# Two heads of q first, setup work moved, weights loaded earlier, and filler matmuls in the early attention units of a fused attention and expert kernel

## The chip, the cores and the metric

The kernel runs on one core of a Trainium2 chip. The metric is the device time of one execution in microseconds. Before the change three runs gave 231.26, 233.02 and 235.55 us; the median, 233.02 us, is the time before. A profile shows one execution, with a span of 231.7 us.

## What is computed

The first half is block attention with 4 batches, 8 heads, 768 rows, 64 columns per head, and 8 blocks of 96 rows. An 8x8 matrix per head is normalised five times (Sinkhorn), and the blocks of k and v are mixed with it. Each block of q then attends to its own mixed block. The second half is a layer of 8 experts: each of the 3072 rows, now 512 wide, goes to one expert.

```python
P = sort_net
for _ in range(5):
    P = exp(P - max(P, -1)); P = P / (sum(P, -1) + 1e-9); P = P / (sum(P, -2) + 1e-9)
k_sorted = einsum('bhij,bhjcd->bhicd', P, k_b)
v_sorted = einsum('bhij,bhjcd->bhicd', P, v_b)
attn = softmax(q_b @ k_sorted.T / 8)            # per block
x = (attn @ v_sorted)                           # rearranged to 3072 x 512
logits = x @ w_gate + modality_bias[modality_id]
e = argmax(logits); gate = max(softmax(logits))
out[row] = gate * (relu(x[row] @ w1[e]) @ w2[e])
```

With the biases of this input, nearly all rows go to two experts. The kernel finds the two likely ones on the chip and handles their rows in slots of 256 rows; whatever is left over goes through a general loop behind a branch.

## The kernel before

The instruction order is fixed by hand: each engine executes what the source issues, in that order. Attention goes in 32 units of four blocks for two batches. Unit `u` does `scores` (8 matmuls into PSUM), `expo` (one exponential on ScalarE), and, one unit later, `av` (8 matmuls, then a division on VectorE into `xb`).

```python
def scores(u):
    g, hf, h = unit(u)
    sc = scpsum.tile([128, 2, 512], FP32, tag="sc", ...)      # one buffer
    for j in range(4):
        for par in range(2):
            nc.tensor.matmul(sc[0:m, par, j * BLK:(j + 1) * BLK], kT[g][rows, x0:x0 + m], qT[rows, i],
                             start=True, stop=True)
def expo(u):
    mark[0] = nc.scalar.activation(attnT[u % 2]..., sc_tiles.pop(u)[0:BLK, :, 0:4 * BLK], ACT.Exp, scale=scale)
def av(u):
    op = opsum.tile([128, 2, 512], FP32, tag="op", ...)       # one buffer
    ...                                                        # 8 matmuls, reciprocal, multiply into xb
```

`BLK` is 96, so the scores use columns 0 to 383 of each of the two 512-column banks. `spread_q` interleaves the q of two heads in SBUF (two copies), `tq_pe` transposes one head on TensorE (6 transposes), and `tq_out` copies the result to `qT`. `sort_k` and `sort_v` do the mixing: matmuls with `bd` (the normalised matrix as a block diagonal), called `ka` and `va` in the profile. Group `g` holds two of the four batches.

The start, and the work between the first units:

```python
    load_q(0, 0)                      # four heads of q
    ...                               # iota, identity
    load_k(0, 0); load_k(0, 1); load_v(0); load_q(0, 1)
    ...
    spread_q(0, 0, nc.gpsimd); spread_q(0, 1, nc.gpsimd)
    ...
    for u in range(4):
        tq_pe(u)
    # five Sinkhorn iterations, make_bd(0), sort_k of group 0
    scores(0); expo(0)
    home_pick(); home_map()           # the two likely experts, on VectorE
    mod_rows()                        # modality ids: a copy, a transpose on TensorE, a copy
    load_k(1, 0); load_k(1, 1)
    wait_w = gate_consts()            # gate weights and biases, mostly on GpSimd
    make_bd(1)
    scores(1); expo(1)
    late_consts()                     # small constants on VectorE
    ...                               # sort_v of group 0 (12 jobs, three in a row: two small, one large)
    load_v(1); load_q(1, 0); load_q(1, 1)
    zero_block(); av(0); wait_w(); prep_s(4)
```

Per group of 8 units, `gate_T` and `gate_L` compute the logits, `choose` the expert, `place` each row's position, and `ones_[m](t)` scatters one set of rows to a DRAM scratch (GpSimd, one indirect DMA each). `table(m)` then works out which slots are ready, and `x_try` loads a slot's rows back with a transposing DMA (`xT`, issued by SyncE). The expert layers run as pieces: `mL1` (8 matmuls of 256 columns, `hp`) and `mL2` (8 matmuls of 512 columns, `yp`). Slots alternate between the two experts.

```python
    at2(9, place, 0)
    for t in range(1, 8):
        at1(9 + t, lambda t: ones_[0](t), t)
        if t == 3:
            at1(9 + t, lambda: load_w(0, parts=(0,)))
    at1(16, table_x, 0)
    at1(16, lambda: load_w(0, parts=(1,)))
    at1(16, lambda: load_w(1))
    ...
    for u in range(2, 32):
        p1, p2 = pace(u)              # (0, 0) before unit 18, then (1, u % 2)
        scores(u); expo(u)
        for f, a in A1.get(u, []): f(*a)
        run_pieces(p1)
        av(u - 1); prep_q(u + 2); prep_s(u + 3)
        for f, a in A2.get(u, []): f(*a)
        run_pieces(p2)
    run_pieces(1); av(31); run_pieces(2); gate_T(3, 3); run_pieces(1); gate_L(3, 3); choose(3)
    run_pieces(2); place(3)
    for t in range(1, 8):
        run_pieces(2); ones_[3](t)
    table_x(3)
    run_pieces(1000)
```

Of the kernel before, what the change touches and what calls it, by code (L numbers as in the profile page):

```python
# [17 lines left out]
def kernel(  # L18
# [13 lines left out]
    nc = tc.nc  # L32
# [58 lines left out]
    def q_in(g, hh):  # L91
        base = q_in1 if g else v_sb[1].rearrange("p x d -> p (x d)")
        return base[:, hh * 3072:(hh + 1) * 3072]
# [19 lines left out]
    def load_v(g):  # L113
        nc.gpsimd.dma_start(out=v_in, in_=v_src[g * 128:(g + 1) * 128])

    def load_q(g, hh):
        t = q_in(g, hh).rearrange("p (r h f) -> p r h f", r=2, h=4)
        return [nc.gpsimd.dma_start(out=t[:, par], in_=q[2 * g + par, 4 * hh:4 * hh + 4]
                                    .rearrange("h (p t) d -> p h (t d)", t=6)) for par in range(2)][0]

    def spread_q(g, hq, eng=None):
        t = q_in(g, hq // 2).rearrange("p (r h t d) -> p r h t d", r=2, h=4, t=6)
        il = q_il[hq % 2].rearrange("p (h t r d) -> p h t r d", h=2, t=6, r=2)
        for z in range(2):
            (eng or nc.vector).tensor_copy(il[:, z], t[:, :, (hq % 2) * 2 + z].rearrange("p r t d -> p t r d"))  # L125
# [1 line left out]
    sI = singles.tile([128, 32], I32)  # L127
    pI = singles.tile([128, 1], I32)
    idI = singles.tile([BLK, NTL], I32)
    load_q(0, 0)  # L130
    nc.gpsimd.iota(sI, pattern=[[1, 32]], base=0, channel_multiplier=0)
    make_identity(nc, ident)
    load_k(0, 0)
    load_k(0, 1)
    load_v(0)
    load_q(0, 1)
    jI = singles.tile([1, 4], I32)
    hI = singles.tile([1, 4], I32)
    nc.gpsimd.iota(pI, pattern=[[0, 1]], base=0, channel_multiplier=1)
# [1 line left out]
    nc.gpsimd.iota(jI, pattern=[[1, 2], [0, 2]], base=0, channel_multiplier=0)  # L141
    nc.gpsimd.iota(hI, pattern=[[PR, 2], [CAP, 2]], base=0, channel_multiplier=0)
    spread_q(0, 0, nc.gpsimd)
    spread_q(0, 1, nc.gpsimd)

    ones_bf = singles.tile([128, 128], BF16)
    ones8 = singles.tile([128, E], FP32)
# [40 lines left out]
    def perm_mult(dst, srcs, nm):  # L188
        eng = nc.gpsimd if nm == "w" else nc.vector
        tmp = small.tile([128, 4, E, E], FP32, tag="ptmp", name=f"ptmp{nm}")  # L190
        a = bass.AP(tensor=srcs.tensor, offset=srcs.offset, ap=[srcs.ap[0], srcs.ap[1], [0, E], srcs.ap[2]])
        p_ = bass.AP(tensor=perm.tensor, offset=perm.offset, ap=[perm.ap[0], [0, 4], perm.ap[1], perm.ap[2]])
        eng.tensor_tensor(tmp, a, p_, ALU.mult)
        return lambda: nc.vector.tensor_reduce(dst, tmp, AX.X, ALU.add)
# [39 lines left out]
    def tq_out(u, eng):  # L234
        g, h = u // 16, u % 8
        qT = qTb[g][:, h * 768:(h + 1) * 768].rearrange("p (i t r) -> p i t r", i=NB, t=6)
        eng(qT, tq.pop(u).rearrange("p t (i r) -> p i t r", r=16))

    for u in range(4):
        tq_pe(u)  # L240
    for it in range(5):
        if it == 0:
            nc.vector.tensor_reduce(red, P_t, AX.X, ALU.max)
            nc.vector.tensor_tensor(P_t, P_t, red.broadcast_to([BH, NB, NB]), ALU.subtract)
        nc.scalar.activation(P_t, P_t, ACT.Exp)
        if it == 3:
            tq_out(0, nc.scalar.copy)
        if it == 4:
            for u in range(1, 4):
                tq_out(u, nc.scalar.copy)  # L250
        for f in gap[it]:
            f()
        nc.vector.tensor_reduce(red, P_t, AX.X, ALU.add)
        nc.vector.reciprocal(red, red)
        nc.vector.tensor_tensor(P_t, P_t, red.broadcast_to([BH, NB, NB]), ALU.mult)
        nc.vector.tensor_reduce(red, P_swap, AX.X, ALU.add)
        nc.vector.reciprocal(red, red)
        colb = bass.AP(tensor=red.tensor, offset=red.offset,
                       ap=[red.ap[0], [0, NB], red.ap[1]])
        nc.vector.tensor_tensor(P_bf if it == 4 else P_t, P_t, colb, ALU.mult)  # L260
# [34 lines left out]
    def mod_rows():  # L295
        src = modI.rearrange("b (r t w) -> b t r w", r=16, t=6)[:, :, :, 0]
        nc.vector.tensor_copy(modB, src)
        tp = mipsum.tile([128, 64], BF16, tag="mi", name="modT")
        nc.tensor.transpose(tp[0:BLK, 0:NTL], modB.rearrange("b t r -> b (t r)"), ident[0:NTL, 0:NTL])
        nc.vector.tensor_copy(modF, tp[0:BLK, 0:NTL])  # L300

    wgf = small.tile([128, 4, E], FP32, tag="wgf", name="wgf")

    def gate_consts():
        red_w = perm_mult(wgf, wg_sb, "w")
        nc.gpsimd.tensor_scalar(modN, modF, -1.0, 1.0, ALU.mult, ALU.add)

        def bb(r):
            t = BTp[0:BLK, r]
            return bass.AP(tensor=t.tensor, offset=t.offset, ap=[t.ap[0], [0, NTL], t.ap[1]])  # L310
        tmp = small.tile([BLK, NTL, E], FP32, tag="btmp", name="btmp")
        nc.gpsimd.tensor_tensor(biasm, modF.broadcast_to([BLK, NTL, E]), bb(1), ALU.mult)
        nc.gpsimd.tensor_tensor(tmp, modN.broadcast_to([BLK, NTL, E]), bb(0), ALU.mult)
        nc.gpsimd.tensor_tensor(biasm, biasm, tmp, ALU.add)

        def rest_w():
            red_w()
            nc.vector.tensor_copy(wgp, wgf)
        return rest_w

    busy = [0.0, 0.0]

# [54 lines left out]
        return u // 16, (u // 8) % 2, u % 8  # L377

    def prep_s(u):
        if 4 <= u < 32 and not (u // 8) % 2 and u % 2 == 0:  # L380
            spread_q(u // 16, (u % 8) // 2)
            use(dve=0.7)

    def prep_q(u):
        if 4 <= u < 32 and not (u // 8) % 2:
            tq_pe(u)
            tq_out(u, nc.scalar.copy if pick(0.8, 0.56) else nc.vector.tensor_copy)

# [2 lines left out]
    def scores(u):  # L391
        g, hf, h = unit(u)
        sc = scpsum.tile([128, 2, 512], FP32, tag="sc", name=f"sc{u}")
        qT = qTb[g][:, h * 768:(h + 1) * 768].rearrange("p (i f) -> p i f", i=NB)
        for j in range(4):
            i = hf * 4 + j
            x0 = (h * 8 + i) * BLK
            m = 128 if h * 8 + i < 63 else BLK
            for par in range(2):
                rows = slice(par * 64, (par + 1) * 64)  # L400
                nc.tensor.matmul(sc[0:m, par, j * BLK:(j + 1) * BLK],  # L401
                                 kT[g][rows, x0:x0 + m], qT[rows, i],
                                 start=True, stop=True)
        sc_tiles[u] = sc

    def expo(u):
        mark[0] = nc.scalar.activation(attnT[u % 2][:, 0:8 * BLK].rearrange("p (r f) -> p r f", r=2),  # L407
# [189 lines left out]
    def zero_block():  # L597
        ins = nc.sync.dma_start(out=xs_dram[ZR:ZR + PR].rearrange("(t p) w -> p t w", t=2), in_=zsrc2)
        in_xs_group(ins.ins)
        pads.append(ins.ins)  # L600
# [8 lines left out]
    def w_views(z):  # L609
        o = z * WCOL  # L610
        return (w01[:, o:o + 4 * F].rearrange("p (c f) -> p c f", c=4),
                w01[:, o + 4 * F:o + WCOL].rearrange("p (c f) -> p c f", c=8))

    def load_w(z, tab=None, n=None, parts=(0, 1)):
        tb, n = (etab, z) if tab is None else (tab, n)
        er = nc.values_load(tb[0:1, n:n + 1], engines=(PoolEng,), min_val=0, max_val=E - 1)
        v1, v2 = w_views(z)
        if 0 in parts:
            nc.gpsimd.dma_start(out=v1, in_=moe_w1[bass.ds(er, 1)].rearrange("o (c p) f -> p (o c) f", p=128))
        if 1 in parts:  # L620
            nc.gpsimd.dma_start(out=v2, in_=moe_w2[bass.ds(er, 1)].rearrange("o (c p) f -> p (o c) f", p=128))

    def stage_of(s):
        return 0 if s < 2 else 1 if s < 4 else 2 if s < 8 else 3
# [123 lines left out]
    expo(0)  # L748
    home_pick()
    home_map()  # L750
    mod_rows()
    load_k(1, 0)
    load_k(1, 1)
    wait_w = gate_consts()
    make_bd(1)
    scores(1)
    expo(1)
    late_consts()
    use(dve=-busy[1], act=-busy[0])
    for n, (f, g, x0, kd) in enumerate(g0[8:]):  # L760
        f(g, x0, kd)
    load_v(1)
    load_q(1, 0)
    load_q(1, 1)
    zero_block()
    av(0)
    wait_w()
    prep_s(4)

    st = {"tab": -1, "x": 0, "l1": 0, "done": 0, "pos": 0}  # L770

# [24 lines left out]
    def at2(u, f, *a):  # L796
        A2.setdefault(u, []).append((f, a))

    at2(8, lambda: nc.vector.memset(v_sb[1][:, :, D:D + 1], 1.0))
    for m in range(4):  # L800
        for c in range(4):
# [3 lines left out]
                at2(u, gate_L, m, c)  # L805
        if m < 3:
            at2(8 * m + 9, choose, m)
    at2(9, place, 0)
    for t in range(1, 8):
        at1(9 + t, lambda t: ones_[0](t), t)  # L810
        if t == 3:
            at1(9 + t, lambda: load_w(0, parts=(0,)))
    at1(16, table_x, 0)
    at1(16, lambda: load_w(0, parts=(1,)))
    at1(16, lambda: load_w(1))
    at1(18, place, 1)
    for t in range(1, 8):
        at2(17 + t, lambda t: ones_[1](t), t)
# [42 lines left out]
    for u in range(2, 32):  # L861
        p1, p2 = pace(u)
        scores(u)
        expo(u)
        for f, a in A1.get(u, []):
            f(*a)
        run_pieces(p1)
        av(u - 1)
        prep_q(u + 2)
        prep_s(u + 3)  # L870
        for f, a in A2.get(u, []):
            f(*a)
        run_pieces(p2)
    run_pieces(1)
    av(31)
    run_pieces(2)
    gate_T(3, 3)
    run_pieces(1)
    gate_L(3, 3)
    choose(3)  # L880
    run_pieces(2)
    place(3)
    for t in range(1, 8):
        run_pieces(2)
        ones_[3](t)
    table_x(3)
    run_pieces(1000)
# [75 lines left out]
```

## Time and profile before

| engine | busy us | share of the span | instructions |
|---|---|---|---|
| TensorE, matmuls | 164.9 | 71% | 2023 |
| TensorE, weight loads | 122.8 | 53% | 2023 |
| VectorE | 104.7 | 45% | 340 |
| ScalarE | 94.3 | 41% | 147 |
| GpSimd | 76.1 | 33% | 102 |

The mean granted TensorE clock is 0.846 of full speed. The core's DMA engines moved 27.67 MB, 119 GB/s over the span. A transposing load of a slot's rows took 3.4 us in the median from issue to landing and 16.0 us at most; a weight load of 1024 KB took 15.8 us in the median.

In the profile the engines are PE (matmuls), PEld (weight loads of TensorE), DVE (VectorE), ACT (ScalarE), POOL (GpSimd) and SP (SyncE); a q after a name means its sequencer. A tile's name tells the stage: `sc` scores, `op` the product with v, `tq` a transpose of q, `gt` and `lg` the gate, `ka` and `va` the mixing, `hp` and `yp` the expert layers, `xs_scratch` the scattered rows. A line of the timeline gives start and duration in us, engine, source line, operation, output and inputs, and in brackets the idle time before it and what ended that. Shares of busy time are averages over stages with different limits, so a stage is read by its own windows.

### The profile page before, as it was taken

To read this page: it belongs to the slowest core of one execution; us is meant where nothing else is said; L and a number is where in the kernel's file an instruction comes from. 1 tells how busy PE (TensorE), PEld (TensorE's weight loads), DVE (VectorE), ACT (ScalarE), POOL (GpSimd) and SP (SyncE) were. 2 spreads that over 40 slices of the span, in tenths; PEclk is the share of its full clock that TensorE was granted. 3 is DMA by queue.
4 is the path that set the end of the run, shared out by engine and by line. 5 is a ranking of instruction groups with operands and counts; after the bars stand their busy time and mean duration, and the time that the engine had idled before them with its cause. 6 is when DMAs were issued, how large, how long until landed. Compare 5 with 4: busy or idle time off the path is not lost.

```text
span 231.7 us, 5104 instructions
## 1 busy us (share of the span) xinstructions
PE 164.9 (71%) x2023; PEld 122.8 (53%) x2023; DVE 104.7 (45%) x340; ACT 94.3 (41%) x147; POOL 76.1 (33%) x102
## 2 busy tenths in 40 slices
PE   0265667995999600298889888999990999999600
PEld 0154565985889500286565657668660576674200
DVE  5868866657548660044566436233270133232100
ACT  2264445665577710075464626443341132322300
POOL 7621515000434420031633465337651031333300
PEclk9997587569569955569999999999998699999965
DMA  5999999990119399981215323594364642212200
GB/s 69 208 228 203 218 213 174 198 184 3 36 36 162 101 150 184 191 138 37 108 48 129 97 75 121 127 145 148 96 214 97 105 103 96 92 45 91 89 15 0
DMA packets 30129, 27.67 MB, mean 119 GB/s; under 512 B 18799, under 2 KB 25743, under 8 KB 29840
## 3 DMA queue, kind: packets, MB, share of 16 engines
q0 software_dynamic: 11760, 23.10, 45.7%
q1 hardware_dynamic: 18336, 4.16, 11.8%
q8 instruction: 18, 0.29, 0.6%
q14 instruction: 15, 0.12, 0.2%
HBM read 27.35 MB, written 10.52 MB: 163 GB/s over the span
## 4 chain that ended last, share of the span: by engine, by line
PE 54%; DVE 16%; DMA 13%; issue 5%; POOL 3%; ACT 2%; SPq 1%; POOLq 0%; DVEq 0%
PE hp L663 19%; PE yp L686 15%; DMA xT<-xs_scratch 10%; PE ka L349 3%; PE gt L433 3%; DVE xb L424 3%; PE va L358 3%; PE op L420 3%; PE sc L401 2%; PE lg L439 2%; DMA xs_scratch<-zpad 2%; PE tq L231 1%; POOL xs_scratch L510 1%; DMA xs_scratch<-xb,dest 1%; DVE v_sb L336 1%
## 5 line engine op out<-in xcount | busy, mean ns | idle before, releaser
L663 PE MATMUL hp<-xT,w 128*128 128x256 bf16 x384 | 50.1, 284 | 18.5 <-DMA xT<-xs_scratch 18.4
L510 POOL DMA_INDIRECT xs_scratch<-xb,dest x32 | 29.6, 925 | 68.5 <-issue 33.6
L663 PEld LDWEIGHTS <-w 128*128 128x128 bf16 x384 | 37.6, 102 | 27.1 <-issue 12.6
L677 POOL DMA_INDIRECT out_dram<-kvb,idg x25 | 24.6, 985 | 54.5 <-ACT kvb L673 27.3
L407 ACT ACTIVATE attnT<-sc 96x768 bf16<-96x768 f32 x32 | 25.8, 806 | 10.8 <-PE sc L401 10.6
L657 ACT ACTIVATE hT<-hp 128x512 bf16<-128x512 f32 x17 | 10.1, 596 | 35.7 <-PE hp L663 35.6
L686 PE MATMUL yp<-w,qT 128*128 128x512 bf16 x96 | 22.9, 383 | 0.0
L424 DVE TENSOR_TENSOR xb<-op,rs 96x512 bf16<-96x512 f32 x32 | 22.0, 687 | 1.7 <-DMA xs_scratch<-xb,dest 0.6
L686 PE MATMUL yp<-w,hT 128*128 128x512 bf16 x96 | 22.5, 379 | 0.0
L423 DVE RECIPROCAL rs<-op 96x8 f32<-96x8 f32 x32 | 6.4, 199 | 30.5 <-PE op L420 29.1
L673 ACT ACTIVATE kvb<-yp,idg 128x512 f32<-128x512 f32 x15 | 10.3, 687 | 21.5 <-PE yp L686 21.5
L231 PE MATMUL tq<-ident,q_il 128*128 128x128 bf16 x96 | 10.8, 270 | 10.7 <-POOL q_il L125 10.3
L420 PE MATMUL op<-v_sb,attnT 96*128 96x65 bf16 x256 | 15.1, 207 | 2.1 <-DVE v_sb L336 1.3
L358 PE MATMUL va<-bd,kvb 128*128 128x128 bf16 x128 | 14.6, 285 | 1.4 <-ACT v_sb L336 0.8
L675 DVE TENSOR_SCALAR kvb<-yp,idg 128x512 f32<-128x512 f32 x9 | 6.8, 751 | 19.5 <-PE yp L686 19.5
L401 PE MATMUL sc<-qT,kT 64*128 64x96 bf16 (+1 forms) x256 | 12.9, 228 | 3.0 <-issue 1.1
L420 PEld LDWEIGHTS <-attnT 96*128 96x128 bf16 x256 | 12.8, 107 | 4.2 <-DVE v_sb L336 1.4
L657 ACT ACTIVATE qT<-hp 128x512 bf16<-128x512 f32 x15 | 9.0, 597 | 14.1 <-PE hp L663 14.0
L336 ACT CAST v_sb<-va 96x512 bf16<-96x512 f32 (+1 forms) x20 | 11.9, 629 | 6.7 <-PE va L358 6.5
L433 PE MATMUL gt<-ident,xb 96*128 96x96 bf16 x128 | 9.8, 230 | 6.6 <-DVE xb L424 5.7
L686 PEld LDWEIGHTS <-qT 128*128 128x128 bf16 x96 | 9.3, 100 | 9.5 <-issue 0.5
L358 PEld LDWEIGHTS <-kvb 128*128 128x128 bf16 x128 | 13.2, 189 | 2.0 <-issue 1.8
(176 smaller groups left out, 213.2 us busy)
## 6 DMA issues: line engine op xcount, KB each, us to landing
w<-in_moe_w_dram POOLq DMA_DIRECT2D x4, 1024.0 KB, 15.8
kvb<-in_k_dram POOLq DMA_DIRECT2D x4, 768.0 KB, 12.1
kvb<-in_v_dram POOLq DMA_DIRECT2D x2, 1536.0 KB, 10.7
v_sb<-in_q_dram POOLq DMA_DIRECT2D x4, 384.0 KB, 14.6
q_in<-in_q_dram POOLq DMA_DIRECT2D x4, 384.0 KB, 13.2
xs_scratch<-zpad SPq DMA_DIRECT2D x3, 258.0 KB, 3.4
xs_scratch<-xb,dest POOLq DMA_INDIRECT x32, 2.6
out_dram<-kvb,idg POOLq DMA_INDIRECT x25, 2.9
```

The lines of the kernel that those rows point to most:

```text
L336: (nc.scalar.copy if pick(act, dve) else nc.vector.tensor_copy)(dst, src)
L358: nc.tensor.matmul(acc[:, z], v_cols[:, d0 + z], bd[g], start=True, stop=True)
L401: nc.tensor.matmul(sc[0:m, par, j * BLK:(j + 1) * BLK], kT[g][rows, x0:x0 + m], qT[rows, i], start=True, stop=True)
L407: mark[0] = nc.scalar.activation(attnT[u % 2][:, 0:8 * BLK].rearrange("p (r f) -> p r f", r=2), sc_tiles.pop(u)[0:BLK, :, 0:4 * BLK], ACT. ...
L420: nc.tensor.matmul(ov[:, par, j], attnT[u % 2][:, c0:c0 + 128], v_sb[g][0:BLK, par * 64 + h * 8 + i, 0:D + 1], start=True, stop=True)
L424: nc.vector.tensor_tensor(xt[:, :, h * D:(h + 1) * D].rearrange("p (r j) d -> p r j d", r=2), ov[0:BLK, :, :, 0:D], rs.broadcast_to([BLK, ...
L433: nc.tensor.transpose(tp[:, t], xb[m % 2][:, t, c * 128:(c + 1) * 128], ident[:BLK, :BLK])
L510: ins = nc.gpsimd.indirect_dma_start(out=xs_dram, out_offset=bass.IndirectOffsetOnAxis(ap=dest[:, t:t + 1], axis=0), in_=xt.bitcast(I32)[: ...
L657: mark[0] = nc.scalar.activation(dst, src, ACT.Relu)
L663: nc.tensor.matmul(hp[:, f], w_at(s, c * F + (2 * j + f) * 128, 128), xT_b[s % NX][:, c], start=(c == 0), stop=(c == 3))
L677: ins = nc.gpsimd.indirect_dma_start(out=out, out_offset=bass.IndirectOffsetOnAxis(ap=idg[:, t, 0:1], axis=0), in_=y, in_offset=None, boun ...
L686: nc.tensor.matmul(yp, hT_b[s % 2][:, fc, t * 128:(t + 1) * 128], w_at(s, 4 * F + fc * Dm, Dm), start=(fc == 0), stop=(fc == 7))
```

## The change

The change reorders the start and the middle, and adds matmuls whose results nothing reads:

- q comes in with two heads, then two, then four. Only two heads are spread and transposed at the start; the others of group 0 are spread on GpSimd between loads.
- The modality rows, the bias constants, the second block diagonal and the late constants move from in front of v's mixing to after it or into units 2 to 4.
- The first expert's weights are loaded before the units. The second expert's loads wait until the rows of slot 1 are in.
- `place(0)`, the scatters of group 0 and `table_x(0)` move by up to one unit; in each unit a piece runs ahead of the gate's work instead of behind it; at the end there is one piece between steps instead of two.
- In units 2 to 17 six matmuls of 128 columns go into columns 384 to 511 of the score tile. They multiply the identity with part of `kT`. They are meant to keep the array active.

```diff
-    load_q(0, 0)
+    load_q(0, 0, 2)
...
-    load_q(0, 1)
+    load_q(0, 2, 2)
+    load_q(0, 4, 4)
...
-    spread_q(0, 1, nc.gpsimd)
...
-    for u in range(4):
+    for u in range(2):
         tq_pe(u)
...
-        if 4 <= u < 32 and not (u // 8) % 2 and u % 2 == 0:
+        if 16 <= u < 32 and not (u // 8) % 2 and u % 2 == 0:
             spread_q(u // 16, (u % 8) // 2)
...
         sc_tiles[u] = sc
+        if 2 <= u < 18:
+            for z in range(6):
+                nc.tensor.matmul(sc[:, z % 2, 4 * BLK:512], ident, kT[0][:, 0:128], start=True, stop=True)
...
     home_map()
-    mod_rows()
     load_k(1, 0)
     load_k(1, 1)
-    wait_w = gate_consts()
-    make_bd(1)
+    wait_w = gate_w()
     scores(1)
     expo(1)
-    late_consts()
...
+    spread_q(0, 1, nc.gpsimd)
     load_v(1)
-    load_q(1, 0)
-    load_q(1, 1)
+    load_q(1, 0, 4)
+    load_w(0, parts=(0,))
+    load_q(1, 4, 4)
+    load_w(0, parts=(1,))
+    spread_q(0, 2, nc.gpsimd)
     zero_block()
+    prep_q(2)
     av(0)
+    prep_q(3)
     wait_w()
-    prep_s(4)
+    mod_rows()
...
+    def late_w1():
+        for i, ins in enumerate(load_w(1)):
+            if i == 0:
+                tc.add_manual_dep(ins.ins, xins[1].ins.name, SYNC, reason="rows of the first slots go ahead")
...
-    at2(9, place, 0)
+    at2(2, lambda: (gate_bias(), spread_q(0, 3, nc.gpsimd)))
+    at2(3, make_bd, 1)
+    at2(4, late_consts)
+    at1(10, place, 0)
     for t in range(1, 8):
-        at1(9 + t, lambda t: ones_[0](t), t)
-        if t == 3:
-            at1(9 + t, lambda: load_w(0, parts=(0,)))
-    at1(16, table_x, 0)
-    at1(16, lambda: load_w(0, parts=(1,)))
-    at1(16, lambda: load_w(1))
+        at2(9 + t, lambda t: ones_[0](t), t)
+    at2(16, table_x, 0)
+    at2(17, late_w1)
...
         expo(u)
+        run_pieces(p1)
         for f, a in A1.get(u, []):
             f(*a)
-        run_pieces(p1)
         av(u - 1)
         prep_q(u + 2)
         prep_s(u + 3)
+        run_pieces(p2)
         for f, a in A2.get(u, []):
             f(*a)
-        run_pieces(p2)
     run_pieces(1)
     av(31)
-    run_pieces(2)
+    run_pieces(1)
     gate_T(3, 3)
...
-    run_pieces(2)
+    run_pieces(1)
     place(3)
     for t in range(1, 8):
-        run_pieces(2)
+        run_pieces(1)
         ones_[3](t)
```

`gate_w` and `gate_bias` are the two halves of `gate_consts`, split.

More of the change, by code (lines that the diff above doesn't have):

```diff
@@ L114, in load_v, with load_q @@
         nc.gpsimd.dma_start(out=v_in, in_=v_src[g * 128:(g + 1) * 128])
[L116 to L119, printed above, removed]
+    def load_q(g, h0, nh):
+        t = q_in(g, h0 // 4).rearrange("p (r h f) -> p r h f", r=2, h=4)
+        z = h0 % 4
+        for par in range(2):
+            nc.gpsimd.dma_start(out=t[:, par, z:z + nh], in_=q[2 * g + par, h0:h0 + nh]
+                                .rearrange("h (p t) d -> p h (t d)", t=6))
     def spread_q(g, hq, eng=None):
@@ L248 @@
         if it == 4:
-            for u in range(1, 4):
-                tq_out(u, nc.scalar.copy)
+            tq_out(1, nc.scalar.copy)
         for f in gap[it]:
@@ L302, with gate_w, rest_w, gate_bias @@
     wgf = small.tile([128, 4, E], FP32, tag="wgf", name="wgf")
-    def gate_consts():
+    def gate_w():
         red_w = perm_mult(wgf, wg_sb, "w")
+        def rest_w():
+            red_w()
+            nc.vector.tensor_copy(wgp, wgf)
+        return rest_w
+    def gate_bias():
         nc.gpsimd.tensor_scalar(modN, modF, -1.0, 1.0, ALU.mult, ALU.add)
@@ L314, in gate_consts @@
         nc.gpsimd.tensor_tensor(biasm, biasm, tmp, ALU.add)
[L316 to L319, printed above, removed]
     busy = [0.0, 0.0]
@@ L384, in prep_q @@
     def prep_q(u):
-        if 4 <= u < 32 and not (u // 8) % 2:
+        if 2 <= u < 32 and not (u // 8) % 2:
             tq_pe(u)
@@ L617, in load_w @@
         v1, v2 = w_views(z)
+        res = []
         if 0 in parts:
-            nc.gpsimd.dma_start(out=v1, in_=moe_w1[bass.ds(er, 1)].rearrange("o (c p) f -> p (o c) f", p=128))
+            res.append(nc.gpsimd.dma_start(out=v1, in_=moe_w1[bass.ds(er, 1)].rearrange("o (c p) f -> p (o c) f", p=128)))
         if 1 in parts:
-            nc.gpsimd.dma_start(out=v2, in_=moe_w2[bass.ds(er, 1)].rearrange("o (c p) f -> p (o c) f", p=128))
+            res.append(nc.gpsimd.dma_start(out=v2, in_=moe_w2[bass.ds(er, 1)].rearrange("o (c p) f -> p (o c) f", p=128)))
+        return res
     def stage_of(s):
```

## The prediction

> **What bounds the kernel now.** I read the page's forty slices first. TensorE is busy 71% of the span, no engine is a plain bound, so the waits decide.
>
> ```profile
> PE   0265667995999600298889888999990999999600
> PEclk9997587569569955569999999999998699999965
> DMA  5999999990119399981215323594364642212200
> ```
>
> Each digit is 5.8 us. TensorE has two holes after the prologue: slices 15 to 16 (from about 84 us) and slice 31 (about 175 to 180 us). In both the clock falls to half, and in the first the DMA row is full. The table of waits names the cause of both, 12.6 us for the longer and, by difference from 18.4 us, 5.8 us for the other:
>
> ```profile
> PE hp L663 <- DMA xT<-xs_scratch: 18.4, 2, 12.6
> ```
>
> The chain of waits shows what stands before each:
>
> ```profile
> 77.86 2.68 DMA xs_scratch<-xb,dest
> 80.75 15.98 DMA xT<-xs_scratch
> 96.86 1.87 PE hp L663 x8
> ...
> 122.54 3.25 DMA xT<-xs_scratch
> ...
> 171.24 3.82 DMA xs_scratch<-zpad
> 175.19 4.67 DMA xT<-xs_scratch
> 179.91 3.59 PE hp L663 x16
> ```
>
> The same transposed load of one slot of rows takes 15.98 us at 80 us and 3.25 us at 122 us. The timeline around 80 us tells why: GpSimd issues three weight loads of 1 MB around it, after one more at 68.23.
>
> ```profile
> 78.91 0.94 POOL L621 DMA_DIRECT2D w<-in_moe_w_dram  x1
> 80.10 0.79 POOL L619 DMA_DIRECT2D w<-in_moe_w_dram  x1 [0.25 <-issue]
> 80.75 1.83 SPq L630 DMA_TRANSPOSE xT<-xs_scratch  x1
> 80.89 1.01 POOL L621 DMA_DIRECT2D w<-in_moe_w_dram  x1
> ```
>
> 3 MB at the 190 GB/s of those windows is 16 us: the rows come with the last of the weights. The second hole is another matter: table 3 is asked for at about 168 us, its pads and rows land at 179.9, twelve us later, and TensorE has work left only until 173.85.
>
> For the attention stage I cut the trace at multiples of 3.413 us from 10.01, because its clock record changes nowhere else:
>
> ```profile
> 40.73:44.14 3.41, 3.41 (x49) 2.90 (x49) 1.88 (x6) 2.74 (x4) 0.00 (x0) 0.50 1.00 203
> 47.56:50.97 3.41, 3.41 (x82) 3.07 (x79) 2.03 (x5) 2.67 (x4) 0.00 (x0) 0.50 1.32 206
> 71.45:74.86 3.41, 3.35 (x59) 3.05 (x57) 3.19 (x7) 2.65 (x5) 1.38 (x2) 1.00 1.12 207
> ```
>
> Columns: length, busy TensorE, weight load, VectorE, ScalarE, GpSimd, then clock. From 37.32 to 50.97 and 57.80 to 68.04 TensorE has no idle time and half a clock; from 68 on it has the full one, and VectorE and ScalarE set the pace.
>
> [...]
>
> **The change, part by part.** Set from the start of unit 4's scores (41.3 us) and of unit 18's (80.6 us).
>
> *Prologue.* Two heads of q instead of four come first, so k lands about 2 us sooner (0.39 MB less at 200 GB/s). But the first ka matmul at 15.57 waited for VectorE's bd, not for k: nothing won. [...] 192 ka at 30.5 ns are 5.9 us against 4.5, about 1 us lost. The modT transpose, which held TensorE until 25.2, moves behind v: 1 to 1.5 us won at the start of va; VectorE also loses 3 us of small work ahead of its v copies. But va hangs on four 16-row jobs that share one PSUM buffer (fill 0.5 to 0.9, copy 1.0 to 1.2, 0.3 between): 8 to 9 us in either kernel. So va ends about 1.2 us earlier, at 32.6. Then a new wait: unit 2 needs heads 4 and 5 spread, now on GpSimd, behind load_v (which waits for va), four q loads and two weight loads: 0.6 + 3.0 + 0.8 + 0.94 with gaps is 6 us, then 0.8 for the first copy, so 39.3. Before, that transpose ran at 37.4. With spreads and biases off VectorE later, I put unit 4 at 42.0: **+0.7**.
>
> *Fillers.* 16 units x 6 = 96 matmuls of 128 columns. Six transposes of the same shape advance the chain by 0.64 us at half clock and 0.34 at full: 107 and 56 ns each, so 10.3 us or 5.4 us of TensorE. In the order of instructions, the signal that the exponential waits for has moved from the last score matmul to the last filler, so they also lengthen the loop scores, exponential, next scores. [...] I take the full clock from about 42 us until the wait.
>
> *Units 4 to 17.* Against before: the half-clock units with k or v work, 5, 7, 6, 11, win 1.3, 0.2, 0.4, 0.75 (their matmuls halve, 0.34 of filler is added); light units 4, 8 and 16 lose 0.1, 0.3, 0.35; unit 13 loses 0.25. Unit 9 held TensorE 2.9 us for choose; place now stands after unit 10's scores, which wins 2.2 and costs 0.8 in unit 10. Table 0 goes behind unit 15's division: 0.5 won in unit 17. Together **-3.5**: scores of 18 at 77.8.
>
> *First rows.* The first expert's weights are loaded from 37 us and are in by about 60 (5.2 MB at 0.2 MB/us); the second's wait for slot 1's rows. From unit 16's exponential: scatter 0.3 + 0.9, landing 2.7, rows 3.3, so 7.2 us, while scores of 18 come 3.8 us after it: a wait of 3.4 to 3.7 us. Before, scores of 18 to the first hp was 96.86 - 80.56 = 16.3. **-12.6**.
>
> *Units 18 to 31.* The piece now precedes gate_T, which waited for VectorE's xb in seven units, like this one:
>
> ```profile
> 107.19 0.51 PE L433 MATMUL gt<-ident,xb 96*128 96x96 bf16 x8 [0.75 <-DVE xb L424]
> ```
>
> 7 x 0.7 = 4.9 won. Place 1, once hidden in the hole, costs 0.9; and slot 2's rows, just in time before, will be waited for by about 1.5. **-2.5**.
>
> *Tail.* Before table 3 the loop runs 21 pieces, then 20; now 11. Nine pieces at (4 x 0.88 + 2 x 1.73) / 6 = 1.17 us are 10.5 us more cover after it, and 5.8 us are needed: the second hole goes. With one piece instead of two, choose and place wait 1.2 us. **-4.8**.
>
> Sum: 0.7 - 3.5 - 12.6 - 2.5 - 4.8 = -22.7, and 233.0 - 22.7 = 210.3: I say **210 us**.
>
> **Rivals.** (1) *The clock does not follow.* If fillers leave it at half, they cost up to 10.3 us where TensorE is the pace: about 217. [...] (2) *A wait takes the first hole's place.* The second expert's 2 MB start after slot 1's rows, about 10.5 us after unit 16's exponential, and take 11; its first use is four units later, at about 20. GpSimd meanwhile stands at that load[...]. If this holds slot 1 or 2 back by 5 us: 215. (3) *GpSimd becomes the prologue's bound*, with seven issues and six copies in order: 3 to 4 us more, 214. (4) *The fillers were for nothing because units are bound by copies*: then units 4 to 17 win nothing, 214. Better than planned: half-clock windows at 97 to 102 gone as well, 3 us, 206.
>
> **Range and chances.** The two holes are 18.4 us of named waits. Each rival is some 4 to 7 us; two at once give about 221, none of them and the extra gain with some luck 201: range 201 to 221. All three rivals together give 226, still below the 228.4 that 2% asks for; only a hole that stays reaches it. Faster by over 2%: 0.94; within 2%: 0.04; slower: 0.02.
>
> **What would show it.** Rows of slot 0 landing 3 to 4 us after their issue, with TensorE idle under 5 us before hp; full clock from about 42 to 78 us; op, scores and tq at full-clock spacing; idle of about 2 us for q_il on GpSimd near 37 us; no idle for xT after table 3. The prediction fails if rows still take over 10 us, if the clock stays at half under the fillers, or if hp waits for w.

## The result, and the profile after

| | before | after |
|---|---|---|
| median, us | 232.97 (231.26 to 235.55) | 217.48 (216.67 to 217.72) |
| ratio | 1 | 0.935, interval 0.929 to 0.941 |
| span of the profiled execution, us | 231.7 | 216.0 |
| mean granted TensorE clock | 0.846 | 0.904 |

Ratios and their intervals, here and in the experiments, are those of the fast executions as recorded and the totals are medians of all, so the two can differ by up to 1% (for e10, 244.65 / 242.51 is 1.009 and the ratio 0.999).

The change wins 15.5 us where the prediction had 22.7. The page after shows where. These are its rows of TensorE, its clock and the DMA engines; a slice is now 5.4 us.

```profile
PE   0218674898979984799994999989999999999200
PEclk9999796559699999599997999999999999999955
DMA  5999999999922112469937033488657612112100
```

The two holes of before, a 0 in the PE row at slices 15 to 16 and at slice 31, are gone: what is left after the prologue is a 4 at slice 16 and a 4 at slice 22. The DMA row is full until slice 11 (59 us) and low after it, so the first expert's weights are in long before the first rows are asked for at 84 us. From 119.8 us on the clock is not lowered until TensorE is done. The table of waits (engine and line, what it waited for: us in total, times, longest) gives the rest of the holes:

```profile
POOL w L626 <- DMA xT<-xs_scratch: 10.4, 1, 10.4
...
PE hp L671 <- DMA xT<-xs_scratch: 6.4, 2, 3.5
```

TensorE now waits 3.5 us for the rows of slot 0 and 2.9 us for those of slot 2, in place of 12.6 and 5.8. A new wait stands on GpSimd: 10.4 us until it may load the second expert's weights (e4 below takes it away). The chain of waits (start, length, what) shows the smaller hole:

```profile
93.25 0.94 POOL w L628
94.70 13.20 DMA xs_scratch<-xb,dest
...
110.39 2.45 DMA xs_scratch<-xb,dest
113.02 3.18 DMA xT<-xs_scratch
116.24 1.78 PE hp L671 x8
```

A scatter behind the second expert's weights lands after 13.20 us, one at 110 us after 2.45 us, and the rows of slot 2 follow it in 3.18.

Milestones of both traces, in us from the start of the span, place the 15.7 us by which the two spans differ. "Exponential 18" is the start of unit 18's exponential; the first hp is the first expert matmul.

| stretch | before | after | difference | predicted |
|---|---|---|---|---|
| to exponential 4 | 41.9 | 44.3 | +2.4 | +0.7 |
| exponential 4 to 18 | 41.5 | 41.6 | +0.1 | -3.5 |
| exponential 18 to the first hp | 13.5 | 1.7 | -11.8 | -12.6 |
| first hp to exponential 31 | 43.5 | 43.2 | -0.3 | -2.5 |
| exponential 31 to the end of TensorE | 77.5 | 70.2 | -7.3 | -4.8 |
| end of TensorE to the end | 13.8 | 15.0 | +1.2 | 0 |

The last four rows together are near the plan (-18.2 against -19.9). The first two, where the fillers stand, are 5.3 us short of it.

These marks flatter the stretch to exponential 18: exponential 4 stands behind six fillers of its own unit, and unit 18 has none. The prediction had set its parts from the starts of the scores of units 4 and 18. There the trace of the kernel before has 41.27 and 80.56 us and that of the change 42.93 and 83.76, so the first three parts are +1.7 (planned +0.7), **+1.6 (planned -3.5)** and -12.5 (planned -12.6). The part that failed is units 4 to 17. These are the change's scores of unit 18 and its first expert matmul:

```profile
83.76 0.34 PE L404 MATMUL sc<-qT,kT 64*128 64x96 bf16 x8
87.58 1.86 PE L671 MATMUL hp<-xT,w 128*128 128x256 bf16 x8 [3.48 <-DMA xT<-xs_scratch]
```

### The profile page after: what moved, and what is told of

It reads as the page before. It is cut to its first block, busy times and chain, and to the rows that moved or that the text cites. A ratio compares the mean times of both kernels' runs of the same rounds, so it can differ in the third digit from the quotient of the medians.

```text
span 216.0 us, 5292 instructions
## 1 busy us (share of the span) xinstructions
PE 165.9 (77%) x2108; PEld 126.8 (59%) x2119; DVE 103.0 (48%) x337; ACT 94.2 (44%) x146; POOL 80.4 (37%) x108
## 4 chain that ended last, share of the span: by engine, by line
PE 55%; DVE 14%; DMA 11%; issue 5%; POOL 5%; ACT 3%; SPq 1%; POOLq 1%; DVEq 0%
PE yp L694 16%; PE hp L671 15%; DMA xs_scratch<-xb,dest 7%; PE va L361 5%; PE ka L352 4%; DMA xT<-xs_scratch 4%; PE sc L410 3%; PE sc L404 3%; PE gt L439 2%; PE lg L445 2%; DVE xb L430 2%; PE op L426 2%; DVE xTg L339 2%; PE tq L233 1%; ACT v_sb L339 1%
## 5 line engine op out<-in xcount | busy, mean ns | idle before, releaser
L671 PE MATMUL hp<-xT,w 128*128 128x256 bf16 x384 | 49.3, 281 | 6.5 <-DMA xT<-xs_scratch 6.4
L413 ACT ACTIVATE attnT<-sc 96x768 bf16<-96x768 f32 x32 | 25.8, 806 | 15.5 <-PE sc L410 10.1
L694 PE MATMUL yp<-w,hT 128*128 128x512 bf16 x90 | 21.9, 379 | 0.4 <-issue 0.2
L683 DVE TENSOR_SCALAR kvb<-yp,idg 128x512 f32<-128x512 f32 x12 | 9.0, 751 | 24.1 <-PE yp L694 20.4
L233 PE MATMUL tq<-ident,q_il 128*128 128x128 bf16 x96 | 10.2, 259 | 10.9 <-POOL q_il L127 10.9
L665 ACT ACTIVATE hT<-hp 128x512 bf16<-128x512 f32 x18 | 10.8, 598 | 17.0 <-PE hp L671 17.0
L665 ACT ACTIVATE qT<-hp 128x512 bf16<-128x512 f32 x17 | 10.1, 597 | 15.6 <-PE hp L671 15.0
L681 ACT ACTIVATE kvb<-yp,idg 128x512 f32<-128x512 f32 x12 | 8.2, 687 | 17.4 <-PE yp L694 17.4
L361 PE MATMUL va<-bd,kvb 128*128 128x128 bf16 x128 | 13.9, 267 | 1.6 <-ACT v_sb L339 1.0
L694 PEld LDWEIGHTS <-hT 128*128 128x128 bf16 x96 | 9.1, 98 | 9.1
L233 PEld LDWEIGHTS <-q_il 128*128 128x128 bf16 x96 | 7.4, 117 | 11.2 <-POOL q_il L127 11.2
```

The costliest lines, as they stand in the source:

```text
L233: nc.tensor.transpose(tp[:, t], src[:, t], ident)
L361: nc.tensor.matmul(acc[:, z], v_cols[:, d0 + z], bd[g], start=True, stop=True)
L665: mark[0] = nc.scalar.activation(dst, src, ACT.Relu)
L671: nc.tensor.matmul(hp[:, f], w_at(s, c * F + (2 * j + f) * 128, 128), xT_b[s % NX][:, c], start=(c == 0), stop=(c == 3))
L694: nc.tensor.matmul(yp, hT_b[s % 2][:, fc, t * 128:(t + 1) * 128], w_at(s, 4 * F + fc * Dm, Dm), start=(fc == 0), stop=(fc == 7))
```

## Experiments

**The question.** The fillers do act on the clock: between exponentials 4 and 18 the half-clock time falls from 21.0 us to 7.5. Yet the stretch is as long as before, and 1.6 us longer at the marks of the plan. Either the fillers pay and something else was lost, or they cost what they bring (the fourth rival). A second question is what holds slot 2 back for 2.9 us, and a third is whether the first hole was really the weights.

The runs came in three sets. e1 to e4 are the first; e5 to e8 and e9 to e12 ran on another chip, on which the kernel before took 245.48 and 242.51 us in the median instead of 232.51. Ratios are always to the kernel before in the same set. At a margin of 2% the comparison with the kernel before is recorded as unclear for e3 and for e5 to e8. Every trace is one execution, and executions of one kernel spread by up to 5% (e10), so a difference of 1 us between two traces is no finding by itself. A letter in an expectation stands for the theory that is spelled out with it.

### e1: the change without the fillers

```diff
-        if 2 <= u < 18:
-            for z in range(6):
-                nc.tensor.matmul(sc[:, z % 2, 4 * BLK:512], ident, kT[0][:, 0:128], start=True, stop=True)
```

> The change without its 96 filler matmuls, all else equal. Theory A (the prediction's account: the fillers pay, since they bring the full clock): the half clock of the kernel before comes back from about 35 to 51 and 58 to 68 us, the stretch from unit 4's exponential to unit 18's grows from 41.6 to about 43.5 us, the time goes from 217.5 to about 219. Theory B (each filler group stands between the scores and their exponential, 0.64 us at half clock and 0.34 at full, and that is more than the clock gives back): the clock falls as under A, but exponential 4 comes about 2 us earlier and the stretch to unit 18 shrinks to 38 to 40 us; time 212 to 215.

Measured: 213.06 us, ratio 0.915 (0.910 to 0.920). The interval lies wholly below that of the change, 0.929 to 0.941: **without the fillers the kernel is 4.4 us faster** (217.48 - 213.06; by the ratios, 0.020 x 232.5, it is 4.7), though the clock of its trace is lower, 0.865 against 0.904. Theory B had the time right, but not the stretch from exponential 4 to 18: 43.2 us where it had 38 to 40. The trace is of the slowest of the six executions, 215.07 us. Its windows view, from unit 8 on (length, busy us of TensorE, weight loads, VectorE, ScalarE, GpSimd, then clock, share of the DMA engines, GB/s), shows the low clock:

```profile
54.10:86.10 32.00, 25.39 (x387) 21.92 (x384) 20.52 (x66) 18.72 (x33) 7.43 (x8) 0.66 0.39 76
```

21.8 of these 32 us are at half clock, and still TensorE is idle for 6.6 us, waiting for others.

### e3: the kernel before, with only the fillers added

```diff
         sc_tiles[u] = sc
+        if 2 <= u < 18:
+            for z in range(6):
+                nc.tensor.matmul(sc[:, z % 2, 4 * BLK:512], ident, kT[0][:, 0:128], start=True, stop=True)
```

> The kernel before with the fillers alone. Theory A: the half clock from 37 to 51 and 58 to 68 us goes, and the time is within 1 us of 233 or 1 us better. Theory B: the clock rises in part of it, and the time is 3 to 5 us longer, 236 to 238.

Measured: 238.35 us against 232.51, ratio 1.022 (1.016 to 1.028). The fillers cost 5 to 6 us in the other order of work too. In the trace the first hp comes at 102.2 instead of 96.9, so 5.3 of the 6.0 us by which its span is longer lie ahead of the first rows, and 3.9 of them between the scores of units 4 and 18 (43.2 us against 39.3).

### e2: the fillers behind the product with v

```diff
         sc_tiles[u] = sc
-        if 2 <= u < 18:
-            ... six fillers
+        sc_keep[u] = sc
...
         av(u - 1)
+        fill(u)
         prep_q(u + 2)
```

> The same 96 fillers, but issued after the unit's product with v, so that the exponential no longer waits for them. If the cost of the fillers is the wait of the exponential, this keeps the clock and loses the delay: 1.5 to 3 us under the change, 214 to 216. If the cost is their time on TensorE, the time stays at 217 to 218. Under theory A it is at or below the version without fillers, under theory B at or above it.

This was to take the fillers out of the way from the scores to the exponential. Measured: 223.24 us, ratio 0.958 (0.953 to 0.963), slower than the change, and neither theory had it. The waits of this run show why:

```profile
PE sc L399 <- ACT attnT L418: 6.3, 12, 1.0
```

L399 is the filler, L418 the exponential. Issued later, the fillers write a tile that the exponential is reading, so they wait for it, 6.3 us in twelve places, and TensorE with them. This run doesn't tell the two theories apart, since it made a wait of its own.

### e5: the fillers in the unused columns of the op tile

```diff
-        if 2 <= u < 18: ... six fillers into sc
...
+        if 1 <= u < 17:
+            for z in range(6):
+                nc.tensor.matmul(op[:, z % 2, 4 * BLK:512], ident, kT[0][:, 0:128], start=True, stop=True)
         for par in range(2):
```

> The same 96 fillers, written into unused columns of the tile of the product with v, just ahead of its eight matmuls, so that they no longer stand between scores and exponential and wait for nothing that the product did not wait for. Without fillers the kernel measured 0.915 of before, with them in the score tile 0.935. Theory B1 (the fillers' cost is the later exponential): about 0.92, 214 us. Theory B2 (it is their time on TensorE, in whatever place, because TensorE in its fixed order holds up everything behind it): 0.93 to 0.94, 216 to 218 us.

Here the exponential doesn't depend on them. Measured: ratio 0.950 (0.942 to 0.958), the first hp at 88.6 us against 87.6 in the change. No gain from freeing the exponential is seen: e7 below, on the same chip with 72 of the 96 fillers in the score tile, is at 0.941. That speaks for B2, that the price is TensorE's time in whatever place. It does not show it, since the change itself was not run on this chip.

### e6 and e7: fillers in units 2 to 5 only, and in 6 to 17 only

```diff
-        if 2 <= u < 18:
+        if 2 <= u < 6:      # e6
+        if 6 <= u < 18:     # e7
```

> Fillers in units 2 to 5 only. There the clock stays at half in spite of them, so each group costs 6 x 107 ns = 0.64 us: 4 x 0.64 = 2.6 us over the version without fillers, 0.926 of before or 215.5 us, if half-clock fillers are the main cost (theory B3). If the cost is spread over all units by count (B4), 24 of 96 fillers cost a quarter of 4.4 us: 1.1 us, 0.92.

> Fillers in units 6 to 17 only, the counterpart. Theory B3: 1.5 to 2 us over the version without fillers, 0.923. B4: 3.3 us, 0.929. If the fillers pay where they bring the full clock (theory A, for these units alone): at or under the version without fillers, 0.912 to 0.915.

Measured: 230.70 us, 0.941 (0.931 to 0.951), and 230.49 us, 0.941 (0.932 to 0.949). The intervals overlap wholly, so the times don't say which units are dear. The traces say more. Exponential 4 starts at 42.9 us in e7 as in e1 (42.9), and at 43.8 in e6 and 44.3 in the change: beside the 42.9, the fillers of units 2 to 4 delay it by 0.9 to 1.4 (by 0.6 in e4, at 43.5). And these are the windows of about the same stretch, exponential 6 to 18, first of e6 (no fillers in it), then of the change (with them):

```profile
49.50:84.40 34.90, 27.46 (x527) 23.85 (x523) 24.16 (x74) 21.94 (x38) 7.46 (x8) 0.79 0.49 91
```

```profile
50.30:85.90 35.60, 28.80 (x595) 25.43 (x591) 23.86 (x74) 22.59 (x37) 7.50 (x8) 0.95 0.45 84
```

A clock of 0.95 instead of 0.79 makes the stretch no shorter, and in e7, on the chip of e6, it takes 37.1 us. TensorE is busy for 1.34 us more in the change than in e6 for all its speed, and is idle some 7 us in both.

### e8: no fillers, and the spread of q ahead of other loads

```diff
     load_v(1)
+    spread_q(0, 2, nc.gpsimd)
     load_q(1, 0, 4)
...
-    spread_q(0, 2, nc.gpsimd)
...
-    mod_rows()
...
-    at2(2, lambda: (gate_bias(), spread_q(0, 3, nc.gpsimd)))
+    at2(2, lambda: (mod_rows(), gate_bias(), spread_q(0, 3, nc.gpsimd)))
```

(The fillers are out as in e1.)

> No fillers, and two waits of the prologue taken out: heads 4 and 5 are spread on GpSimd right after the v load is issued, ahead of the q and weight loads, and the modality transpose goes to unit 2. In the trace without fillers TensorE stood 2.3 us for the spread and 1.4 us for the transpose. If these waits are on the path: 3 to 3.7 us under the version without fillers, 0.90 of before, 209 to 210 us. If the next wait takes their place (exponential 2, the late division by VectorE): 1 us or less, 212.

Measured: 227.51 us, 0.931 (0.924 to 0.939), beside 0.941 for e6 and e7, with overlapping intervals. In e12, below, the change without fillers is at 0.942 on this chip. Exponential 4 starts at 41.3 us, 1.6 earlier than in e1 and 1.5 earlier than in e12, so the two moves together (the spread and the modality rows) shorten the prologue by about that much. Unit 8 starts only 0.2 us earlier than in e1 (53.9 and 54.1): the win is lost again in units 4 to 7, of which 10.4 us run at half clock against 4.3.

### e12: the change without the fillers, on the second chip

> The version without fillers once more, as the neighbour of the three others on the same chip. It measured 0.915 of before; the same ratio is expected within the interval, 0.91 to 0.92, and the trace again at half clock for 30 us or more between 20 and 80 us.

The kernel is that of e1. Measured: 228.16 us, 0.942 (0.936 to 0.949), a smaller win than its 0.915 on the first chip. No run of the changed kernel itself stands beside it there, so the 4.4 us rest on the runs in which the kernel before took 232.5 to 233.0 us. On the second chip e5, with all 96 fillers, is at 0.950, and e6 and e7, with a part of them, are at 0.941, in another set: there the loss by the fillers is not shown.

### What the fillers cost and what they bring

All traces together give a sum. Between exponentials 8 and 18, with the us of half clock in that stretch:

| no fillers there | us | half clock | fillers there | us | half clock |
|---|---|---|---|---|---|
| before | 29.9 | 12.0 | after | 29.0 | 1.7 |
| e6 | 29.2 | 14.8 | e4 | 29.8 | 3.4 |
| e12 | 29.5 | 12.8 | e3 | 31.7 | 7.8 |
| e8 | 30.2 | 12.0 | e7 | 31.3 | 7.9 |
| e10 | 30.9 | 16.5 | e5 | 31.0 | 8.3 |
| e1 | 32.0 | 21.8 | | | |
| e9 | 32.4 | 22.4 | | | |
| mean | 30.6 | 16.0 | mean | 30.6 | 5.8 |

(e2 is left out for its own wait, and e11, whose stages are moved.) With the fillers there are 10.2 us of half clock less, and the stretch is as long. A straight line through the twelve, with one step for the fillers, has 0.27 us for each us of half clock and 2.8 us for the fillers of these ten units; it misses the points by 0.5 us on average, by 1.1 at most. As an estimate, 10.2 x 0.27 = 2.8 us won and 2.8 paid. The marks hide some of the price here too, since exponential 8 stands behind fillers and exponential 18 does not. And the line shows that the two go together, not which is the cause. Were TensorE the pace all the time, a us at half clock would cost about 0.5: six transposes of q advance the chain by 0.64 us at half clock (39.90 to 40.54 in the kernel before) and by 0.34 at full (71.21 to 71.55), so the same work takes 0.53 of the time. 0.27, if it is the effect of the clock, means that about half of the time others set it.

Ahead of unit 8 there is nothing to set against the cost. Exponential 8 starts at 57.0, 55.1 and 55.9 us in the change, e4 and e5, and at 54.1, 54.2 and 53.9 in e1, e12 and e8: on average 1.9 us later. The first hp is later by the same 1.9 us on average (87.6, 86.2 and 88.6 against 86.9, 84.6 and 85.1). The other 2.5 of the 4.4 us are not placed by these traces.

### e4: the second expert's weights in unit 2

```diff
-    at2(2, lambda: (gate_bias(), spread_q(0, 3, nc.gpsimd)))
+    at2(2, lambda: (gate_bias(), spread_q(0, 3, nc.gpsimd), load_w(1)))
...
-    at2(17, late_w1)
```

> The change with the second expert's weights loaded in unit 2, behind the first expert's, without the wait for slot 1's rows. Theory C (the late load is what delays the scatters of group 1: GpSimd waits 10.4 us for it and one scatter takes 13.2 us to land behind 2 MB of weights): the scatters go at one per unit, the 2.9 us wait for slot 2's rows at 113 us and the half clock after it go, time 212.5 to 214.5. Theory D (slot 2's rows are late because table 1 stands only in unit 24): the wait stays at 2 to 3 us, time 216.5 to 218.

Measured: 217.57 us, 0.935 (0.930 to 0.941), as the change; its six executions spread from 213.72 to 218.75, two of them below all of the change's, so the times alone don't tell C from D. The trace, of the fastest execution, does. The edit takes away GpSimd's 10.4 us and the load before the second group's scatters, and the wait for slot 2 stays almost as long (total, times, longest; the longest is slot 0's, the other 2.4 us slot 2's):

```profile
PE hp L671 <- DMA xT<-xs_scratch: 5.8, 2, 3.4
```

So the 13.20 us of the scatter in the chain above are not what holds slot 2 back. Of the two theories the place of table 1, in unit 24, is what remains; e11 moves it.

### e11: everything that seemed to help

No fillers, e8's prologue, e4's weights, the second group's scatters two to a unit and table 1 a unit earlier:

```diff
-        at2(17 + t, lambda t: ones_[1](t), t)
-    at2(24, table_x, 1)
+        (at2 if t % 2 else at1)(19 + t // 2, lambda t: ones_[1](t), t)
+    at1(23, table_x, 1)
```

> No fillers; heads 4 and 5 spread ahead of the q and weight loads; the modality transpose in unit 2; the second expert's weights in unit 2; the scatters of group 1 two in one unit and table 1 in unit 23. If the waits named in the traces (2.3 and 1.4 us in the prologue, 2.2 us for slot 2's rows) are on the path: 4 to 6 us under the version without fillers. If each only gives way to the next one: 1 to 2 us.

Measured: 230.55 us, 0.947 (0.940 to 0.955), beside 0.942 for e12 in the same set: not better. The wait for slot 2 is gone from the waits, and another stands near it, before the first use of slot 2's rows at 116.9 us (113.2 in e12):

```profile
PE lg L442 <- DVE tb_ti L559: 3.3, 2, 2.8
```

The gate now waits for VectorE, which works on the table (tb_ti). So slot 2's wait did hang on the place of table 1, and the wait only changed its owner.

### e9: the kernel before with all expert weights loaded in the prologue

```diff
     load_q(1, 1)
+    load_w(0)
+    load_w(1)
...
-        if t == 3:
-            at1(9 + t, lambda: load_w(0, parts=(0,)))
-    at1(16, lambda: load_w(0, parts=(1,)))
-    at1(16, lambda: load_w(1))
```

> The kernel before with one part of the change: both experts' weights are loaded behind group 1's q, ahead of the units, instead of in units 12 and 16. Theory H (the weights alone make the first rows late): slot 0's rows land 3 to 4 us after their issue instead of 16, the 12.6 us wait falls to under 2 us since the place step still holds TensorE before it, and the time falls by 11 to 13 us, ratio 0.945 to 0.955. Rival: the rows wait for the last scatter or the table as well, the wait falls by half or less, ratio 0.97.

Measured: 232.04 us against 242.51, 0.953 (0.944 to 0.961), so **-10.5 us for the loads alone** (-11.5 by the ratio). The timeline of this run, where the first rows come (start, us, engine, line, operation):

```profile
83.30 1.35 SPq L630 DMA_TRANSPOSE xT<-xs_scratch  x1
...
86.68 1.65 PE L663 MATMUL hp<-xT,w 128*128 128x256 bf16 x7
```

The load of a slot's rows that took 15.98 us in the kernel before is done at most 3.4 us after its issue, and no wait for it stands before hp: its table of waits has only the second hole, 5.5 us, left. This is the first hole's cause, shown alone.

### e10: the kernel before with one piece between the steps of the tail

```diff
-    run_pieces(2)
+    run_pieces(1)      # after av(31), before place(3), and in the loop over t
```

> The kernel before with another part of the change: one piece instead of two between the last steps. Prediction's account: nine pieces more are left after table 3, the 5.8 us wait at 174 us goes and about 1.2 us of waits for choose and place come: 4.8 us, ratio 0.98. In the trace of the change the time from unit 31's exponential to TensorE's end fell by 7.3 us: ratio 0.97 if all of that is the tail's.

Measured: 244.65 us, 0.999 (0.994 to 1.004): nothing in the total. In its trace the edit does what was planned. The count for table 3 (`cp`) comes 19.2 us after exponential 31 (165.7 against 146.5), where it is 27.5 in the kernel before, 28.9 in e9 on this chip, and 18.6 in the change. No wait for the rows of table 3 is left. Instead, TensorE stops 3.2 us for a count on VectorE:

```profile
165.68 0.17 PE L538 MATMUL cp<-ohs,ones_bf 96*128 96x8 bf16 x1
...
170.80 2.51 PE L663 MATMUL hp<-xT,w 128*128 128x256 bf16 x11 [3.18 <-DVE cnt L552]
```

And the gate waits 3.5 us at 142.5. On this chip the kernels show stops of 1 to 4 us after 130 us that the first chip's traces don't have. The trace is of the fastest of 22 executions, 238.31 us; why the median shows no gain stays open, and the edit alone wasn't tried on the first chip.

## Why the prediction was right and wrong

**First rows: right.** Planned: a wait of 3.4 to 3.7 us in place of 12.6. Measured: 3.5, and from the scores of unit 18 to the first hp -12.5 of 12.6. e9 shows the cause: the rows came late because the weights were loaded at the same time. A slot's rows took 16.0 us from issue to landing beside 3 MB of weights in the kernel before, and at most 3.4 without them in e9.

**Tail: right in direction, too small.** -7.3 against -4.8. The windows of both kernels from exponential 31 to TensorE's end, before and then after, give the missing term:

```profile
140.40:217.90 77.50, 70.29 (x508) 46.34 (x508) 24.41 (x76) 24.71 (x40) 27.03 (x30) 0.96 0.44 111
```

```profile
130.80:201.00 70.20, 68.00 (x500) 45.22 (x506) 24.46 (x76) 24.41 (x40) 27.72 (x31) 1.00 0.47 124
```

Idle time falls from 7.2 to 2.2 us (77.50 - 70.29, 70.20 - 68.00), which is the hole less what small waits came: 5.0, as planned. Another 2.3 us are in the busy time of nearly the same matmuls. The hole had come with 6.8 us of half clock, from 177.3 to 184.1, of which TensorE worked 4.2 us, from 179.9 on; about half of these, 2.1 us, is an estimate of their cost (16 hp advance the chain by 3.38 us from 179.91 on, and by 1.75 at full clock from 170.49 on). The plan had counted the hole and not the slow stretch after it. Table 3's count comes sooner in the change (149.4 instead of 167.9), and e10 shows that the single pieces at the end do that by themselves; that they shorten the total is not shown, since the total of e10 did not fall.

**Units 4 to 17, the fillers: wrong, and this is the step that failed.** At the plan's own marks these units take 1.6 us more, where 3.5 less were planned. Of the 3.5, the plan's terms give 1.6 to the fillers (2.65 won where "their matmuls halve", 1.0 lost) and 1.9 to the moves of place and of table 0. The prediction took "the full clock from about 42 us". In the change's trace it came at 48.1, and half clock came back from 54.9 to 58.3. The windows (after the length, TensorE, weight loads, VectorE, ScalarE, GpSimd, clock):

```profile
37.85:41.27 3.42, 2.73 (x33) 2.40 (x34) 0.95 (x3) 0.63 (x1) 3.34 (x6) 0.50 1.00 214
41.27:44.68 3.41, 3.41 (x47) 3.19 (x45) 2.19 (x8) 1.38 (x3) 1.67 (x3) 0.50 1.07 176
44.68:48.09 3.41, 3.41 (x42) 2.89 (x39) 2.27 (x12) 2.70 (x4) 0.22 (x1) 0.50 1.23 210
```

These are the last 10.24 us before the clock rose. Fillers run in all three (at 39.72, 43.36 and 45.63 us), and the clock is 0.50 throughout: that it would be full from 42 us on was the author's estimate, and what raised it at 48.1 is not shown. At half clock the unit grows by the fillers themselves:

```profile
39.72 0.82 PE L410 MATMUL sc<-kT,ident 128*128 128x128 bf16 x6
...
40.64 0.81 ACT L413 ACTIVATE attnT<-sc 96x768 bf16<-96x768 f32 x1 [2.94 <-PE sc L410]
```

In the timeline, six fillers run until 40.54, and the exponential, idle for 2.94 us, starts 0.1 later. The next operation starts 0.62 us after them (40.34), as the prediction's 0.64 has it for half clock.

But the late clock is not the whole of it. In e4's trace, with the same fillers, the clock is full from 42.14 us until 59.2, near the 42 of the prediction. First that stretch, then the one from exponential 4 to 18:

```profile
42.14:59.21 17.07, 13.13 (x370) 11.56 (x370) 11.60 (x36) 11.32 (x17) 2.59 (x4) 1.00 1.22 203
43.50:84.90 41.40, 33.11 (x714) 29.34 (x710) 27.65 (x89) 27.38 (x45) 8.97 (x12) 0.96 0.88 160
```

With 3.4 us of half clock instead of the 21.0 of the kernel before, the stretch takes 41.4 us, as before. So what failed is the value that the plan gave to the clock: it did not make the units shorter by more than the fillers cost. From the scores of unit 4 to those of 18 the change, e4 and e5 take 40.7 us on average, and e1, e12 and e8, without fillers, 39.0: the fillers cost 1.7 there where they were to win 1.6, and their cost in the whole kernel is the 4.4 us of e1 (each trace is a single execution, so 1.7 is an estimate).

Whether the 1.9 of the moves came stays open: by the scores the three without fillers are 1.8 shorter than the kernel before, e9 and e10 (40.8), by the exponentials only 0.2 (42.3 and 42.6), and e1 and the kernel before, both on the first chip, differ by 0.5 the other way.

The fourth rival had said that units 4 to 17 would win nothing, and that came. Its reason, that copies bound the units, is not shown: in the two long windows of e6 and the change above VectorE is busy for 24 of 35 us and ScalarE for 22 to 23.

Two readings on which the plan rested were loose. Its windows show VectorE and ScalarE at 3.19 and 2.65 of 3.41 us from 71.45 on and TensorE at 3.35, so that the first two "set the pace" there is not shown. And "no idle time" holds from 40.73 to 50.97; in the three windows from 37.32, 57.80 and 61.21 TensorE is busy for 3.16 to 3.21 of 3.41 us.

Nor did a busy TensorE mean the full clock here: the second and third of the change's windows above, 6.82 us together, show it busy throughout at a clock of 0.50.

**Prologue: the order right, the fillers missing.** +2.4 to exponential 4, +1.7 to the scores of unit 4, against +0.7. Without fillers in units 2 to 4 exponential 4 starts at 42.9 (e1, e7), +1.0. The 1.4 us above it are fillers at half clock (0.50 from 34.4 to 48.1 us): the prologue's sum has no term for them. GpSimd's late spread, foreseen at 39.3, came at 38.5, with TensorE idle for 1.3 us. ka took 5.25 us: the plan's 5.9 was its estimate at half clock, and the kernel before has 4.49.

**Units 18 to 31: the gate's wait won, the rest given back.** The waits for xb before gate_T fell from 5.7 us to 0.6, near the 4.9 planned. But the wait for slot 2 was 2.9, not 1.5, and 8.3 us of half clock (to 92.5, and 116.4 to 119.8) stand against 5.3 before. The second rival had seen the hold and blamed the second expert's weights; e4 shows that it was not them.

**The last row**, +1.2 after TensorE's end, is not explained. The other traces have 13.5 to 14.8 us there, without a pattern that the edits explain; the change has 15.0.

The fastest kernel measured is the change without its fillers, 213.06 us on the first chip.

## What to carry to other kernels

Before loading weights, look for what must come in while they do: here a slot's rows took 16.0 us beside 3 MB of weights and at most 3.4 without them, and the loads moved forward in e9 were worth 10.5 us by themselves. Padding matmuls can raise the clock and still lose: here the mean clock is 0.904 with them and 0.865 without, and they cost 4.4 us in one order of work and 5 to 6 in another. So run the change without them before keeping them, and value a faster clock only where TensorE sets the pace. A hole in TensorE's work can also be followed by a slow clock (here 4.2 us of work at half clock), so count both.

## What the runs showed that was not expected

- One us of half clock went with 0.27 us in units 8 to 17, about half of the 0.5 that it would cost if TensorE set the pace (by the 0.64 and 0.34 us of six transposes). This is an estimate from twelve single executions.
- One kernel's times and its mean clock go together. Six executions of e4 had spans of 212.1 us at a mean clock of 0.929, 213.9 at 0.907, 215.4 at 0.900, 216.4 at 0.892, 216.5 at 0.893 and 217.1 at 0.892. Which of the two follows from the other is not shown, and what sets them wasn't tried.
- The same kernel took 232.5 us on one chip and 242.5 to 245.5 on another. Up to the first hp the second chip's traces are no longer (the same kernel has it at 86.9 in e1 and at 84.6 in e12); from there to TensorE's end they are (124.4 in e12, 111.9 in e1). The cause stays open.
- A matmul into columns that nobody reads is not free of the tile's readers: in twelve places they waited, 6.3 us in all, for an exponential that reads other columns (e2).
